# Two of four start-up transposes leave TensorE for the DMA queue, and two sets of weight sums change their place

## The chip, the cores and the metric

The kernel runs on one core of a Trainium2 chip. A core has five engines that run on their own and wait for each other by semaphores: TensorE (PE, matrix products, with a separate record PEld for its weight loads), VectorE (DVE), ScalarE (ACT), GpSimd (POOL) and SyncE (SP), which in this kernel does nothing but issue DMA transfers. Sixteen DMA engines carry out what the queues issue. The metric is the device time of one execution in microseconds (us). Before the change the median of seven runs is 655.6 us (654.49 to 656.85).

## The reference

One input x of 2048 rows (tokens) and 1024 columns goes through two branches that are mixed by a gate per token.

```python
x = A_x
g = _sigmoid((x * gate_w).sum(-1, keepdims=True))
a = _A_ref(x, A_wqkv, A_wo)
b = _B_ref(x, B_w_in, B_w_sp, B_b_sp, B_w_out)
return g * a + (1 - g) * b
```

Branch A is attention with 32 heads of 32 columns, in which a token sees eight tokens only: itself and those 2, 4, ... 14 places before it.

```python
qkv = (x @ wqkv).reshape(B, S, 3, H, Dh).transpose(2, 0, 3, 1, 4)
logits = jnp.einsum('bhsd,bhswd->bhsw', q, kg) * scale
attn = _softmax(logits, axis=-1)
o = jnp.einsum('bhsw,bhswd->bhsd', attn, vg)
return o.transpose(0, 2, 1, 3).reshape(B, S, D) @ wo
```

Branch B is a gated MLP of 3584 hidden columns, whose second half z2 is normalized and mixed over all tokens by the 2048x2048 matrix w_sp.

```python
z = _gelu(jnp.einsum('bsd,df->bsf', x, w_in))
z1 = z[..., :Fh]
z2 = _layernorm(z[..., Fh:], axis=-1)
g = jnp.einsum('ts,bsf->btf', w_sp, z2) + b_sp[None, :, None]
return jnp.einsum('bsf,fd->bsd', z1 * g, w_out)
```

## The kernel before

**Tiles.** A tile of x is 128 tokens; there are sixteen. Nearly every product needs x with its 1024 columns along the partitions, so x is kept turned, as xT: eight blocks of 128 columns by 2048 tokens. A tile reaches xT in one of two ways. A plain load puts it in the buffer xn, TensorE turns its eight 128x128 blocks (`xpose`, L221: eight transposes, and eight copies out of PSUM, in turn on ScalarE L228 and VectorE L230). Or a transposing load (L179, `dma_start_transpose`) writes it turned. Before the change tiles 0 to 3 go the first way and 4 to 15 the second.

**Start.** ScalarE's queue loads the gate's vector gw and the first quarter of wvp, the weights of v for the first three head groups. All else is on SP's queue, in an order that `chained` (L155) fixes: x tile 0, the other three quarters of wvp, x tiles 1 to 3, the transposing loads of tiles 4 and 5, the q and k weights of head group 0 (`load_wqk(0)`), the transposing loads of tiles 6 to 15, `load_wqk(1)`, zeros for the rows ahead of v. All later transfers of SP stand behind these (the proxy at L188). TensorE meanwhile multiplies a cleared buffer six times (`keep_warm`), turns gw into an extra column of wvp, does two more such products, turns tile 0, and runs `vp_tile` (L299) for tiles 0 to 3: eight products of 128x385 that make v and the gate's sum. The turning of the next tile stands inside the product before it (`middle`). Then come `qk_tile` (L290) for 512 tokens at a time, which needs four tiles and the q and k weights, `vp_tile` for further tiles, and small products for the bands of logits (L356, copied by ScalarE at L364). The bands are stored to DRAM by SP and read back in another layout (`load_bands`, L650) for the softmax on VectorE: the maxima L671 to L674, the exponential L662 on ScalarE, weights L683 to L692, then products with v (four slices L708) and their sums L712 to L717.

**Strassen products.** From the gate (L406) on most products are quads: a 2x2 block product in seven products instead of eight (Winograd's form). Their generators are `strassen` (L438) and `chain` (L499), their products line L435. Each needs four sums of weight blocks, made on VectorE (`sums4_steps`, L574, recorded as L577). Between the seven products ScalarE seeds one bank from another (L518) and copies a result to SBUF (L524), and VectorE adds two results (`plus`, L506). Two quads run in step.

**The order of the work.** In the live part a planner writes the order down. It keeps a modelled clock for each engine and each DMA, and at every step `advance(t)` (L764) emits the pieces of other work that are due: pending transfers, exponentials, and on VectorE the earliest among the streams maxima, weights, products, and the list `fill` of sums. A piece of `fill` is due at a modelled time, for instance a modelled landing plus `LATE` = 0.5. On the chip every engine runs its instructions in the order written (`settle`, L211). The planner's clocks start with fixed values at L1001 to L1009.

**The steps that the change touches.** The z2 half of w_in is loaded in two sets (`load_later`, L988; eight pairs of loads each), and when the planner has the last of them landed, four sums go to `fill` at L994. The first set is read by quads at about 186 us, the second by quads some 35 us later. The z1 half runs as seven steps `fp` (loop at L1200), each of two quads; `load_w1` (L841) loads two halves f of w1 for the steps fp and fp + 1 together, `w1_sums` (L1146) makes their sums one step ahead. At the end of a step each quad stores its results (`store`, L1170). In steps 2 to 4 `RAW_AT` places transposing loads of w_sp (`load_raw`, L1109) between the products; eight of them make the first half, and VectorE's sums L1126 to L1130 read all eight.

Of the kernel before, what the change touches and what calls it, by code (L numbers as in the profile page):

```python
# [27 lines left out]
ZC = 448  # L28
# [30 lines left out]
def kernel(  # L59
# [60 lines left out]
    xn = reg(R_OFF, 4 * D).rearrange("p (i d) -> p i d", i=4)  # L120
# [40 lines left out]
    def first_dma(o, i):  # L161
        return chained(nc.sync.dma_start(o, i))

    def load_wqk(g, dma):
        for t in range(2):
            dma(wqk_slots[g][:, t], wq_v[:, :, t * D + g * C:t * D + (g + 1) * C])

    nc.scalar.dma_start(gw_s[:], gw_v)
    def load_wvp(k, dma):
        dma(wvp[:, k:k + 2, 0:VP], wq_v[:, k:k + 2, 2 * D:2 * D + VP])  # L170

    load_wvp(0, nc.scalar.dma_start)
    first_dma(xn[:, 0:1, :], x_v[:, 0:1, :])
    for k in range(2, KT, 2):
        load_wvp(k, first_dma)
    for i in range(1, 4):
        first_dma(xn[:, i:i + 1, :], x_v[:, i:i + 1, :])
    for i in range(4, 16):
        chained(nc.sync.dma_start_transpose(xT[:, :, i * P:(i + 1) * P], x2[i * P:(i + 1) * P, :]))  # L179
        if i == 5:  # L180
            load_wqk(0, first_dma)
    load_wqk(1, first_dma)
    first_dma(bass.AP(tensor=v_d.tensor, offset=v_d.offset, ap=[[C, 16], [(S + 16) * C, NG], [1, C]]), zeros)
# [133 lines left out]
    def keep_warm(n):  # L317
        for _ in range(n):
            inst = nc.tensor.matmul(banks[7], warm[:, 0:P], warm, start=True, stop=True, skip_group_check=True)
            pinned.setdefault(inst.ins.engine, inst.ins.name)  # L320

    keep_warm(6)
    gwT = banks[1][:, 0:KT // 2].bitcast(BF)
    nc.tensor.transpose(gwT, gw_s[:], ident[0:KT, 0:KT])
    nc.vector.tensor_copy(wvp[:, :, VP:VP + 1], gwT.rearrange("p (k o) -> p k o", o=1))
    keep_warm(2)
    xpose(0)
    for i in range(4):
        vp_tile(i, middle=lambda: xpose(i + 1) if i < 3 else None)
    band_at = [0]  # L330
    last_sub = [None]
    last_evac = [None]
# [306 lines left out]
        sync.dma_start(v_t, bass.AP(tensor=v_d.tensor, offset=v_d.offset + (g * (S + 16) + 2) * C, ap=[[NJ * C, P], [1, NJJ * C]]))  # L639


    FR, LATE = 0.4, 0.5
    t_bands, t_v = [FAR] * NG, [FAR] * NG
    sub_end, exp_end = [FAR] * NG, [FAR] * NG
    v_data = [0.0]
# [97 lines left out]
    weighed, fill = [0], []  # L743
# [64 lines left out]
    def wz_sums(p):  # L808
        w = wz[p]
        return sums4_steps(wzs[p], w[0][:, 0:4], w[0][:, 4:8], w[1][:, 0:4], w[1][:, 4:8])  # L810
# [27 lines left out]
    def w1_half(fp, f):  # L838
        return w1_first[:, f] if fp == 0 else w1_pairs[(fp - 1) // 2 % 2][f][:, :, (fp - 1) % 2 * P:((fp - 1) % 2 + 1) * P]

    def load_w1(fp):  # L841
        for f in range(2):
            to = w1_first[:, f] if fp == 0 else w1_pairs[(fp - 1) // 2 % 2][f]
            sync.dma_start(to, win_v[:, :, HF * f + fp * P:HF * f + (fp + (2 if fp else 1)) * P])

# [142 lines left out]
    def load_later(p, at, gap):  # L988
        land = [0.0]

        def landed(t):
            land[0] += 1
            if land[0] == KT:
                fill.extend((t + LATE, 1.05, f) for f in wz_sums(p))  # L994
        for n, f in enumerate(load_wz(p)):
            dma(at + gap * n, 0.65, f, landed, True)

# [143 lines left out]
    z1s_slots = [[free(o + 2048 * r, 2048).rearrange("p (f a t) -> p f a t", f=2, a=2) for r in range(2)] for o in (T1_OFF, R_OFF + 16384)]  # L1141
    zv_slots = [free(R_OFF + 20480 + 1024 * r, 1024, F32) for r in range(2)]

    w1_left = [0]

    def w1_sums(fp):  # L1146
        def one(f):
# [10 lines left out]
    def z1_quad(fp, c):  # L1158
        a, b, s = w1_half(fp, 0), w1_half(fp, 1), ws_slots[fp % 2]
        z1s, vs = z1s_slots[fp == 3][c], zv_slots[c]  # L1160
        lo, hi = slice(512 * c, 512 * c + 512), slice(1024 + 512 * c, 1536 + 512 * c)

        def share(*a):
            last_share[0] = nc.vector.tensor_copy(*a)

        def gelu(f, a, bank):
            act(0.6 + table("gelu"), max(clock["PE"], clock["DVE"] if f + a == 2 else 0.0) + 0.2)
            last_gelu[0] = nc.scalar.activation(z1s[:, f, a, :], bank[:], ACT.Gelu_apprx_tanh)  # L1168

        def store():  # L1170
            dst = z1_d[c].rearrange("p (f t) -> p f t", f=NF)[:, fp:fp + NFH + 1:NFH, :]
            last_store[0] = sync.dma_start(dst, z1s.rearrange("p f a t -> p f (a t)"))

        return chain([a[:, k] for k in K4], [a[:, 4 + k] for k in K4], [b[:, 4 + k] for k in K4],
                     *[[s[:, q, k, :] for k in K4] for q in range(4)],
                     [xT[:, k, lo] for k in K4], [xT[:, 4 + k, lo] for k in K4], [xT[:, 4 + k, hi] for k in K4],
                     *[[x[:, k, lo] for k in K4] for x in xts], vs, gelu, nc.scalar.copy if fp < 2 else share, 512, lean=True, done=store)
# [18 lines left out]
    dma(clock["PE"] + 1.0, 2.9, lambda: load_w1(1), w1_landed(1))  # L1196
    RAW_IN = 3.0
    DRAIN, SUMS = 1, NFH - 2
    RAW_AT = {2: {2: 0, 4: 1, 6: 2}, 3: {4: 3, 6: 4}, 4: {2: 5, 4: 6, 6: 7}}
    for fp in range(NFH):  # L1200
        while w1_left[0]:
            advance(max(clock["PE"], clock["DVE"]) + 0.5)
        if 0 < fp < NFH - 1:
            w1_sums(fp + 1)
        if fp == SUMS:
            fill.extend((clock["PE"] + RAW_IN, 1.15, f) for f in wsp_sums(0, 0))
        late = () if fp else [b[2] for b in bank_roles]
        at = [0]
        run(z1_quad(fp, 0), z1_quad(fp, 1), hooks={3: lambda: mark(late, 512, ZC), **{n: lambda a=a: load_raw(0, a) for n, a in RAW_AT.get(fp, {}).items()}},
            step=lambda: z1_step(fp, at))  # L1210
        if fp == DRAIN:
            drain()
        if fp in (0, 2):
            load_w1(fp + 3)
        if fp == NFH - 3:
            load_rows()
    while fill:
# [426 lines left out]
```

## Time and profile before

| what | value |
|---|---|
| median of seven runs | 655.6 us |
| the profiled execution: its time, its span | 654.91 us, 653.1 us |
| granted TensorE clock | 1.00 in the whole span |
| TensorE busy / waits after the first 2 us | 645.0 us / 3.2 us |
| VectorE busy from 56 to 300 us | nearly all of it; from 80 to 164 it is 78.0 of 84 us |
| share of the chain that ended last | PE 87%, DVE 5%, ACT 4%, DMA 1% |

The span runs from the first to the last instruction, and the execution's own time lies 1.8 us above it. A row of the timeline gives start, length, engine, line of the kernel, operation, out<-in with shapes, a count (merged rows), and in brackets the idle time before it with the work that ended it. A row of an SPq gives the time that SP's sequencer spent on issuing; the transfer lands later. In a list of waits the numbers are the total in us, how often, and the longest.

### The profile page before, as it was taken

Reading aid. Unit: us, or ns where it says so; the run is one execution under the profiler, and the core shown is the slowest. Engines: PE = TensorE matmul, PEld = TensorE weight load, DVE = VectorE, ACT = ScalarE, POOL = GpSimd, SP = SyncE. Lnnn points to the kernel's source line nnn. Section 1 sums busy time; section 2 is a strip of 40 time slices with the busy share of each in tenths; the row PEclk is TensorE's granted clock in tenths of the full one; section 3 lists DMA queues with packets and bytes.
Section 4 is the critical chain, followed back from the end, with each engine's and each line's share of the span. In section 5 each row is a group of like instructions: output and inputs, shape, how many; then the busy total and the mean of one; then the engine's idle time right before and its main releaser. Section 6 shows DMA issues by size and latency. Waiting matters only on the chain.

```text
span 653.1 us, 11411 instructions
## 1 busy us (share of the span) xinstructions
PE 645.0 (99%) x4425; PEld 339.0 (52%) x4425; DVE 517.8 (79%) x820; ACT 298.4 (46%) x652; POOL 6.2 (1%) x15
## 2 busy tenths in 40 slices
PE   8999999999989999999999999999999999999998
PEld 4544467544445555444444444444444444868684
DVE  2533989999899999999898776977659999586862
ACT  4545677766677787799554112111121112202020
POOL 1000000000000000001000000000000000000000
PEclk9999999999999999999999999999999999999999
DMA  9989545697768004247995568559487473455601
GB/s 218 189 212 233 111 101 151 149 232 171 180 181 230 6 1 125 65 129 204 285 222 177 124 161 179 131 160 284 116 187 172 98 152 90 115 143 112 132 30 52
DMA packets 230198, 98.19 MB, mean 150 GB/s; under 512 B 177520, under 2 KB 217088, under 8 KB 230144
## 3 DMA queue, kind: packets, MB, share of 16 engines
q1 hardware_dynamic: 229856, 97.27, 60.8%
q8 instruction: 34, 0.56, 0.4%
q10 hardware_dynamic: 288, 0.20, 0.1%
q14 instruction: 20, 0.16, 0.1%
HBM read 45.10 MB, written 36.61 MB: 125 GB/s over the span
## 4 chain that ended last, share of the span: by engine, by line
PE 87%; DVE 5%; ACT 4%; DMA 1%; issue 1%; SPq 0%; DVEq 0%; ACTq 0%
PE psum_all L435 68%; PE psum_all L1468 8%; PE psum_all L294 7%; PE psum_all L304 3%; ACT arena L870 1%; DVE arena L708 1%; PE psum_all L356 1%; ACT arena L1168 1%; DMA arena<-in_B_w_in_dram 1%; DVE arena L577 1%; DVE psum_all L506 1%; DMA arena<-in_A_x_dram 1%; DVE arena L712 1%; ACT arena L364 0%; ACT arena L815 0%
## 5 line engine op out<-in xcount | busy, mean ns | idle before, releaser
L435 PE MATMUL psum_all<-arena 128*128 128x512 f16 (+6 forms) x2462 | 493.0, 362 | 2.6 <-DVE psum_all L506 1.5
L435 PEld LDWEIGHTS <-arena 128*128 128x128 f16 (+1 forms) x2462 | 239.8, 98 | 248.2 <-issue 4.4
L708 DVE TENSOR_TENSOR arena<-arena,att_A 128x2048 f16<-128x2048 bf16 x64 | 75.2, 1218 | 0.3
L294 PE MATMUL psum_all<-arena 128*128 128x512 bf16 x256 | 57.5, 379 | 0.0
L506 DVE TENSOR_TENSOR psum_all<-psum_all,arena 128x512 f32<-128x512 f32 (+1 forms) x74 | 48.1, 667 | 7.4 <-PE psum_all L435 5.1
L1468 PE MATMUL psum_all<-arena 128*128 128x256 f16 (+1 forms) x468 | 51.7, 273 | 0.0
L1468 PEld LDWEIGHTS <-arena 128*128 128x128 f16 x468 | 45.8, 98 | 5.7 <-issue 0.2
L453 ACT COPY psum_all<-psum_all 128x512 f32<-128x512 f32 (+1 forms) x24 | 12.5, 519 | 67.1 <-PE psum_all L435 66.4
L815 ACT ACTIVATE arena<-psum_all 128x448 bf16<-128x448 f32 x64 | 34.3, 545 | 18.5 <-PE psum_all L435 9.0
L1168 ACT ACTIVATE arena<-psum_all 128x512 bf16<-128x512 f32 x56 | 31.1, 615 | 20.8 <-PE psum_all L435 12.7
L294 PEld LDWEIGHTS <-arena 128*128 128x128 bf16 x256 | 24.4, 98 | 28.4 <-issue 0.2
L712 DVE TENSOR_TENSOR arena<-arena 128x2048 f16<-128x2048 f16 x32 | 38.0, 1216 | 0.0
L364 ACT CAST arena<-psum_all 128x1988 f16<-128x1988 f32 (+3 forms) x25 | 34.0, 1359 | 2.8 <-PE psum_all L356 2.4
L870 ACT ACTIVATE arena<-arena 128x896 bf16<-128x896 bf16 x32 | 30.9, 980 | 0.0
L297 ACT CAST arena<-psum_all 128x512 bf16<-128x512 f32 x32 | 18.8, 586 | 26.5 <-PE psum_all L294 26.4
L577 DVE TENSOR_TENSOR arena<-arena 128x512 f16<-128x512 bf16 (+3 forms) x52 | 25.5, 522 | 5.8 <-DMA arena<-in_B_w_in_dram 5.3
L477 ACT COPY psum_all<-psum_all 128x512 f32<-128x512 f32 (+1 forms) x24 | 12.3, 518 | 37.4 <-PE psum_all L435 36.8
L581 DVE TENSOR_TENSOR arena<-arena 128x1024 f16<-128x1024 f16 (+2 forms) x17 | 12.1, 719 | 19.1 <-PE psum_all L435 15.7
L459 ACT COPY arena<-psum_all 128x512 f32<-128x512 f32 (+1 forms) x24 | 12.7, 533 | 25.1 <-PE psum_all L435 22.8
L464 ACT COPY psum_all<-psum_all 128x512 f32<-128x512 f32 (+1 forms) x24 | 12.4, 517 | 25.8 <-PE psum_all L435 24.8
L518 ACT COPY psum_all<-psum_all 128x512 f32<-128x512 f32 (+1 forms) x37 | 20.6, 567 | 5.7 <-PE psum_all L435 5.0
L304 PE MATMUL psum_all<-arena 128*128 128x385 bf16 x128 | 22.6, 327 | 0.0
(112 smaller groups left out, 521.6 us busy)
## 6 DMA issues: line engine op xcount, KB each, us to landing
arena<-v_d SPq DMA_DIRECT2D x8, 960.0 KB, 6.3
z_d<-arena SPq DMA_DIRECT2D x14, 512.0 KB, 4.3
arena<-z_d SPq DMA_DIRECT2D x14, 512.0 KB, 4.1
zg_d<-arena SPq DMA_DIRECT2D x56, 128.0 KB, 2.2
arena<-zg_d SPq DMA_DIRECT2D x32, 224.0 KB, 3.3
band_d<-arena SPq DMA_DIRECT2D x28, 248.5 KB, 4.0
arena<-in_A_wqkv_dram SPq DMA_DIRECT2D x16, 256.0 KB, 4.6
o_d<-arena SPq DMA_DIRECT2D x4, 1024.0 KB, 6.1
```

Of the source, the lines that this page charges most:

```text
L294: nc.tensor.matmul(ps[:], w[:, t, kt, :], xT[:, kt, 512 * c:512 * (c + 1)], start=(kt == 0), stop=(kt == KT - 1))
L304: nc.tensor.matmul(ps[:, 0:VP + 1], xT[:, kt, i * P:(i + 1) * P], wvp[:, kt, :], start=(kt == 0), stop=(kt == KT - 1))
L364: nc.scalar.copy(dst, src)
L435: nc.tensor.matmul(bank[:, 0:N], lhsT, rhs, start=(start and m == 0), stop=(m == n - 1), skip_group_check=True)
L506: last_add[0] = nc.vector.tensor_tensor(out[:, n], a[:, n], vs, ALU.add)
L577: return [lambda a=a: nc.vector.tensor_tensor(*a) for a in args]
L708: lambda ws=ws, in0=in0, in1=in1: tt(p5[:, ws], in0[:, ws], in1[:, ws], ALU.mult)), False
L712: lambda a=p3[:, ws], b=p3[:, ws.start + 4:ws.stop + 4]: tt(a, a, b, ALU.add)), not n
L815: nc.scalar.activation(z2[:, i + 8 * a, ZC * c:ZC * (c + 1)], bank[:, 0:ZC], ACT.Gelu_apprx_tanh, accum_out=s1[:, 4 * n + c:4 * n + c + 1])
L870: return nc.scalar.activation(junk, src, ACT.Square, accum_out=(s2, s2h)[x][:, n:n + 1])
L1168: last_gelu[0] = nc.scalar.activation(z1s[:, f, a, :], bank[:], ACT.Gelu_apprx_tanh)
L1468: nc.tensor.matmul(bank[:, h], l, r, start=(start and m == 0), stop=(m == len(ab) - 1), skip_group_check=True)
```

## The change

- Only tiles 0 and 1 are loaded plainly and turned by TensorE. Both loads stand ahead of the three quarters of wvp on SP's queue. Tiles 2 and 3 become transposing loads, ahead of the others, and `load_wqk(0)` follows tile 3 instead of tile 5.
- On TensorE tile 0 is turned right after the six warm products, then gw, then tile 1; the two further warm products are gone, and nothing stands inside the first products.
- The z2 sums are due 4.0 after the modelled landing instead of 0.5 (`WZ_LATE`).
- `load_w1(5)` is issued in two parts: half 0 ahead of the sixth product of step 2, half 1 after the step and ahead of that step's two stores, which are kept until then. The transposing load of w_sp number 2 moves from step 2 to step 3, which now has numbers 2, 3 and 4.

```diff
+    PLAIN = 2
     nc.scalar.dma_start(gw_s[:], gw_v)
...
     load_wvp(0, nc.scalar.dma_start)
     first_dma(xn[:, 0:1, :], x_v[:, 0:1, :])
+    first_dma(xn[:, 1:2, :], x_v[:, 1:2, :])
     for k in range(2, KT, 2):
         load_wvp(k, first_dma)
-    for i in range(1, 4):
-        first_dma(xn[:, i:i + 1, :], x_v[:, i:i + 1, :])
-    for i in range(4, 16):
+    for i in range(PLAIN, 16):
         chained(nc.sync.dma_start_transpose(xT[:, :, i * P:(i + 1) * P], x2[i * P:(i + 1) * P, :]))
-        if i == 5:
+        if i == 3:
             load_wqk(0, first_dma)
...
     keep_warm(6)
+    xpose(0)
     gwT = banks[1][:, 0:KT // 2].bitcast(BF)
     nc.tensor.transpose(gwT, gw_s[:], ident[0:KT, 0:KT])
     nc.vector.tensor_copy(wvp[:, :, VP:VP + 1], gwT.rearrange("p (k o) -> p k o", o=1))
-    keep_warm(2)
-    xpose(0)
+    xpose(1)
     for i in range(4):
-        vp_tile(i, middle=lambda: xpose(i + 1) if i < 3 else None)
+        vp_tile(i, middle=None)
...
-    FR, LATE = 0.4, 0.5
+    FR, LATE, WZ_LATE = 0.4, 0.5, 4.0
...
-    def load_w1(fp):
-        for f in range(2):
+    def load_w1(fp, halves=(0, 1)):
+        for f in halves:
...
-                fill.extend((t + LATE, 1.05, f) for f in wz_sums(p))
+                fill.extend((t + WZ_LATE, 1.05, f) for f in wz_sums(p))
...
-    w1_left = [0]
+    w1_left, kept_stores = [0], []
...
-        def store():
+        def store(now=False):
+            if fp == 2 and not now:
+                kept_stores.append(store)
+                return
             dst = z1_d[c].rearrange("p (f t) -> p f t", f=NF)[:, fp:fp + NFH + 1:NFH, :]
...
-    RAW_AT = {2: {2: 0, 4: 1, 6: 2}, 3: {4: 3, 6: 4}, 4: {2: 5, 4: 6, 6: 7}}
+    RAW_AT = {2: {2: 0, 4: 1}, 3: {2: 2, 4: 3, 6: 4}, 4: {2: 5, 4: 6, 6: 7}}
...
-        run(z1_quad(fp, 0), z1_quad(fp, 1), hooks={3: lambda: mark(late, 512, ZC), **{n: lambda a=a: load_raw(0, a) for n, a in RAW_AT.get(fp, {}).items()}},
-            step=lambda: z1_step(fp, at))
+        hooks = {3: lambda: mark(late, 512, ZC), **{n: lambda a=a: load_raw(0, a) for n, a in RAW_AT.get(fp, {}).items()}}
+        if fp == 2:
+            hooks[6] = lambda: load_w1(5, (0,))
+        run(z1_quad(fp, 0), z1_quad(fp, 1), hooks=hooks, step=lambda: z1_step(fp, at))
         if fp == DRAIN:
             drain()
-        if fp in (0, 2):
-            load_w1(fp + 3)
+        if fp == 0:
+            load_w1(3)
+        if fp == 2:
+            load_w1(5, (1,))
+            for f in kept_stores:
+                f(True)
```

## The prediction

> **What bounds the kernel now.** I read the page first, then the waits of TensorE, then the start and the two waits that the change names in the timeline.
>
> ```profile
> span 653.1 us, 11411 instructions
> PE 645.0 (99%) x4425; PEld 339.0 (52%) x4425; DVE 517.8 (79%) x820; ACT 298.4 (46%) x652; POOL 6.2 (1%) x15
> ...
> PE 87%; DVE 5%; ACT 4%; DMA 1%; issue 1%; SPq 0%; DVEq 0%; ACTq 0%
> ```
>
> TensorE is busy 99% of the span, so only its own work and its own waits can shorten the run. The waits of TensorE:
>
> ```profile
> PE psum_all L435 <- DVE psum_all L506: 1.5, 2, 1.4
> PE psum_all L319 <- DVE arena L314: 1.2, 1, 1.2
> PE psum_all L356 <- ACT arena L364: 0.8, 2, 0.6
> PE psum_all L435 <- ACT arena L903: 0.6, 1, 0.6
> PE psum_all L435 <- ACT psum_all L518: 0.3, 1, 0.3
> ```
>
> There are 3.2 us after the start: the most that mended waits can return. The start, in the timeline:
>
> ```profile
> 3.98 1.03 PE L319 MATMUL psum_all<-arena 128*128 128x512 bf16 x2
> ...
> 4.15 3.89 SPq L179 DMA_TRANSPOSE arena<-in_A_x_dram  x2
> ...
> 9.34 15.16 SPq L179 DMA_TRANSPOSE arena<-in_A_x_dram  x10
> ...
> 10.24 0.91 PE L225 MATMUL psum_all<-ident,arena 128*128 128x128 bf16 x8
> ...
> 52.37 1.29 SPq L190 DMA_DIRECT2D att_L<-band_d  x2
> ...
> 56.17 0.29 DVE L671 TENSOR_TENSOR att_m<-att_L 128x256 f16<-128x256 f16 x1 [7.21 <-DMA att_L<-band_d]
> ...
> 59.37 0.63 ACT L662 ACTIVATE att_L<-att_L 128x512 f16<-128x512 f16 x1
> ```
>
> The reader should see SP, not TensorE, as the late one here: from 0.7 to 60.5 us SP issues almost without a gap, and VectorE idles 7.21 us for a load that SP issues at 52.37. The two named waits, and what TensorE pays for each:
>
> ```profile
> 167.40 1.23 DVE L708 TENSOR_TENSOR arena<-arena,att_A 128x2048 f16<-128x2048 bf16 x1
> ...
> 171.41 2.22 DVE L577 TENSOR_TENSOR arena<-arena 128x1792 f16<-128x1792 bf16 x2 [2.79 <-DMA arena<-in_B_w_in_dram]
> ...
> 193.83 6.40 PE L435 MATMUL psum_all<-arena 128*128 128x448 f16 x33 [1.36 <-DVE psum_all L506]
> ...
> 319.27 1.56 DVE L577 TENSOR_TENSOR arena<-arena 128x512 f16<-128x512 bf16 x4 [2.46 <-DMA arena<-in_B_w_in_dram]
> ...
> 323.99 8.36 PE L435 MATMUL psum_all<-arena 128*128 128x512 f16 x38 [0.18 <-DVE psum_all L506]
> ```
>
> **The change, part by part.** The sum is made against the profiled execution: 654.91 us, its span 653.1, 0.7 below the median 655.6.
>
> *TensorE at the start.* Two groups of eight transposes go, 0.69 us from first start to the next line's start (6.85 to 7.54, 8.20 to 8.89): 1.4. Two warm matmuls go (3.98 to 4.80): 0.8. The wait for x tile 1 (6.57 to 6.85) goes: 0.3. Sixteen copies of 0.21 us on ScalarE and VectorE go too; both idle there, so they count nothing. ScalarE's queue keeps its two loads, and POOL's issues none before or after. What is late next are the last weight rows: their load is now behind x tile 1, whose own load landed at 6.8 (issue 2.69 plus 4.1), and they take its place, 0.2 after they are needed. The gate transpose moved behind the first tile hides its 0.19 us copy under the second tile's transposes. Lead: 1.4 + 0.8 + 0.3 - 0.2 = 2.2-2.3; I take 2.2. The transposing loads must keep up: tile 2 issued at 3.2 and landing 5.0 later (the row of tile 4) is there at 8.2, needed at 8.4; tile 3 at 9.1 to 9.9, needed at 9.7; the first q and k weights, issued 1.0 earlier, at 10.6 and 12, needed at 11.1 and 12.8. A slip of up to 1.5 us is covered by what follows.
>
> *SP at the start, which decides.* SP loses two plain issues (0.51 and 0.48 from start to start) and gains two transposing ones (1.35 in the steady stretch 16.4 to 24.5): 2.7 - 1.0 = 1.7 us later at everything behind them: wqk 1, the zeros, the v and band stores, the wvr and wqk 2 loads, the loads of the first group's bands. On the way one wait of SP, 0.6 us for the band copy L364 at 38, falls away because TensorE leads. So the band load, and VectorE's L671, come 1.1 us later: L674 ends at 57.41 + 1.1 = 58.5, and the exponential L662 can start at 58.6. It has 59.37 now, because ScalarE is busy for TensorE until then. Behind it in ScalarE's order stands L518 (59.90), the copy that seeds the bank for the third product: TensorE waits for it. So of the 2.2 only 59.37 - 58.6 = **0.7 us** gets past 60 us. Bounds: if both new transposing loads issue as the slowest did (2.49), SP is 4.1 later, 3.5 after the 0.6, and the start loses 1.7; if the shorter plain backlog saves the 2.9 us by which five early transposing issues exceed 1.31, SP is earlier than now and the whole 2.2 passes. I take 0.7, from the steady row: nine of the twelve issues lie nearer to it than to 2.49.
>
> In these rows a transposing load of one x tile holds SP for 1.31 us, a plain one for 0.41 to 0.47. [...]
>
> *The z2 sums.* They are entered 3.5 us later in the planner's list (4.0 for 0.5 after the modelled landing). Work from its other streams takes their place: three slices of L708 (3.49 for three) and the maxima L671 to L674. The weights land at 171.3; sums placed after 168.6 + 3.5 find them, so the 2.79 wait goes. What is late next is the next group's band load: its second half is issued at 169.8 and lands 2.4 later, 172.2. After two slices (170.9) the maxima wait 1.3. VectorE gains 2.79 - 1.3 = 1.5; TensorE had stopped at 192.47 (187.01 + 5.46) and can take back only its **1.36**. Bounds: 0.4 if the maxima come after one slice, 1.36 if nothing waits. I take 1.35, the nearer. The second set of sums (four near 1.08, 210.3 to 215.8) moves by as much, to 219 at most; its first is read by the second product of the first quad of the second set, near 220.8 (the additions of that round start at 223.79, two steps of 1.5 later). That margin is its cover.
>
> *The w1 loads.* The two loads for the sixth step (0.98 and 1.36 to issue, landing 6.1 and 6.8 later) pass two stores (1.2) and one transposing load of the spatial weights (2.1), issuing at 307.9 in place of 311.4: they land by 316 and the 2.46 wait at 316.8 goes. TensorE gets its **0.18**. The stores wait longer; their slots are reused two steps on. The spatial load moved a step on has the same issues ahead of the last one as now, so the sums L1126 at 335.9 keep a margin of about 1 us (last landing 332.9 less 3.84, plus 5.8). If that cover goes, VectorE waits for up to one such issue, 2.1.
>
> *After that.* From 194 to 324 TensorE waits 0.5 in all, and ScalarE waits 7.7 us for TensorE between 194 and 262, so the others follow an earlier TensorE; from 324 to the end it has no wait. Sum: 0.7 + 1.35 + 0.2 = **2.25 us**: 652.7 for the profiled run, **653.4** for the median. Own range, with the start between 0 and 1.5 and the sums between 0.9 and 1.36: 652.4 to 654.5.
>
> The six warm matmuls of 512 columns take 2.74 us, 0.46 each; from 5.6 on matmuls of 385 columns start 0.16 apart. The granted clock in the profile's rows is 1.00 all the while. [...]
>
> **The rivals.**
> 1. SP is not late: 0.7 becomes 2.2, time 655.6 - 3.75 = 651.9. For it: the early long issues follow plain loads, of which there are fewer. Against: transfers keep the DMA share near 1.0 from 4 to 28 us, and two more transposing loads do not lessen that.
> 2. The wait changes its name: the maxima stand ahead of the slices and wait for the band load, 0.4 for 1.35: 655.6 - 1.3 = 654.3.
> 3. SP at its worst: 1.35 + 0.2 - 1.7 = -0.15: 655.7. For it: the second transposing issue took 2.49, and now it stands where both do.
> 4. Slower: the second set of z2 sums, 3.5 later, falls among the additions L506 of the next quads, and TensorE waits behind each: up to 4 x 1.08 = 4.3, 655.6 - 2.25 + 4.3 = 657.7. From 2.25 on it decides the sign. For it: VectorE has 1.0 us of waits between 200 and 256. Against: the margin of several us above.
>
> **How the numbers follow.** A difference of 0.2% (1.3 us) is about what a measurement here can tell from none. Forecast 0.50 (0.44 of it faster), rival 1 0.12, rival 2 0.13 (half and half at the bound), rival 3 0.10 (same, a little slower), rival 4 0.15. Faster 0.60, same 0.23, slower 0.17. The range takes in rivals 1 to 3 with a margin for the reordered list: 651.7 to 656.4; rival 4 stays out.
>
> **What would show it.** Right: the L294 matmuls start near 11.1 rather than 13.3; L671 near 57.3 and L662 near 58.6, with ScalarE idle ahead of it; no DMA wait of L577 near 171 and 319, perhaps one of L671 near 172; no wait of TensorE near 193. Wrong: L662 after 59.4, TensorE idle before 15, or a new wait on L506 after 210.

## The result, and the profile after

The changed kernel takes **652.99 us** in the median of 15 runs (650.85 to 654.33). The kernel before, run beside it on the same chip, takes 655.45 us (36 runs). The ratio is 0.9959, with a 95% interval of 0.9950 to 0.9967: 2.5 us faster. The profiled execution of the changed kernel took 652.99 us, with a span of 651.2 us (before: 654.91 and 653.1).

The head of the page and the summary of its chain of waits:

```profile
span 651.2 us, 11356 instructions
PE 643.6 (99%) x4407; PEld 338.1 (52%) x4407; DVE 516.1 (79%) x812; ACT 296.5 (46%) x644; POOL 6.2 (1%) x15
...
PE 85%; DVE 5%; ACT 5%; DMA 3%; issue 1%; SPq 1%; DVEq 0%; ACTq 0%
```

TensorE is still what bounds the kernel. Its busy time fell by 1.4 us (18 matmuls and transposes fewer), and DMA now has 3% of the chain in place of 1%. Two of the waits of TensorE after the change moved by more than 0.1 us (total, times, longest):

```profile
PE psum_all L435 <- ACT psum_all L518: 0.8, 2, 0.5
...
PE psum_all L435 <- DVE psum_all L506: 0.6, 1, 0.6
```

The wait on L506, VectorE's addition, fell from 1.5 to 0.6. The wait on L518, ScalarE's seeding copy, rose from 0.3 to 0.8. The rows that say where both come from are in the timeline, first the opening stage:

```profile
11.29 2.97 PE L294 MATMUL psum_all<-arena 128*128 128x512 bf16 x13
...
53.22 1.28 SPq L190 DMA_DIRECT2D att_L<-band_d  x2
...
56.98 0.29 DVE L671 TENSOR_TENSOR att_m<-att_L 128x256 f16<-128x256 f16 x1 [7.58 <-DMA att_L<-band_d]
...
58.25 0.63 ACT L662 ACTIVATE att_L<-att_L 128x512 f16<-128x512 f16 x1 [0.77 <-DVE att_L L674]
58.79 0.58 ACT L518 COPY psum_all<-psum_all 128x512 f32<-128x512 f32 x1
...
59.42 1.02 PE L435 MATMUL psum_all<-arena 128*128 128x512 f16 x4 [0.52 <-ACT psum_all L518]
60.37 0.65 PE L356 MATMUL psum_all<-arena 32*64 32x71 bf16 x56
```

The two rows of the kernel before that these are held against:

```profile
13.28 2.97 PE L294 MATMUL psum_all<-arena 128*128 128x512 bf16 x13
...
61.67 0.65 PE L356 MATMUL psum_all<-arena 32*64 32x71 bf16 x56
```

The q and k products start at 11.29 in place of 13.28, so TensorE leads by 1.99 us. The load of att_L, however, is issued 0.85 us later than before. VectorE's maxima follow at 56.98, ScalarE idles 0.77 us for them before the exponential L662, and L518 stands behind that. TensorE waits 0.52 us there; the band product L356 starts at 60.37 in place of 61.67. **1.3 us of the 2.0 pass.** From there to 186 us the lead stays at 1.3.

The stage of the z2 sums, timeline and then chain of waits (start, length):

```profile
166.78 2.36 DVE L708 TENSOR_TENSOR arena<-arena,att_A 128x2048 f16<-128x2048 bf16 x2
...
171.67 0.29 DVE L671 TENSOR_TENSOR att_m<-att_L 128x256 f16<-128x256 f16 x1 [2.53 <-DMA att_L<-band_d]
...
173.96 4.22 DVE L577 TENSOR_TENSOR arena<-arena 128x1792 f16<-128x1792 bf16 x4
...
191.15 1.16 DVE L506 TENSOR_TENSOR psum_all<-psum_all,arena 128x448 f32<-128x448 f32 x2
...
191.82 5.38 PE L435 MATMUL psum_all<-arena 128*128 128x448 f16 x26 [0.65 <-DVE psum_all L506]
...
192.21 2.35 DVE L712 TENSOR_TENSOR arena<-arena 128x2048 f16<-128x2048 f16 x2
```

```profile
163.08 6.07 DMA band_d<-arena
...
169.21 2.38 DMA att_L<-band_d
```

VectorE's rows before the change, for the same additions L506:

```profile
192.02 1.22 DVE L712 TENSOR_TENSOR arena<-arena 128x2048 f16<-128x2048 f16 x1
193.15 1.16 DVE L506 TENSOR_TENSOR psum_all<-psum_all,arena 128x448 f32<-128x448 f32 x2
```

The sums L577 no longer wait, but VectorE still does: 2.53 us for the band load where it waited 2.79 us for the weights. The wait changed its name. Yet TensorE goes on at 191.82 in place of 193.83, 2.0 us ahead of before. Then 0.3 us is given back, because two slices of L712 now stand ahead of the next pair of L506: at 262 us TensorE is 1.7 ahead. The wait of 0.18 on L506 near 324, behind the w1 sums, is gone. The last step of the kernel is 1.95 us earlier (650.12 to 648.17). So 1.3 from the start, 0.7 at 192 us, 0.3 given back and 0.2 at 324 us make 1.9, which is what the two profiled executions differ by; their medians differ by 2.5.

### The profile page after: what moved, and what is told of

The parts are those of the page before. It is cut to its first block, busy times and chain, and to the rows that moved or that the text cites. A ratio compares the mean times of both kernels' runs of the same rounds, so it can differ in the third digit from the quotient of the medians.

```text
span 651.2 us, 11356 instructions
## 1 busy us (share of the span) xinstructions
PE 643.6 (99%) x4407; PEld 338.1 (52%) x4407; DVE 516.1 (79%) x812; ACT 296.5 (46%) x644; POOL 6.2 (1%) x15
## 4 chain that ended last, share of the span: by engine, by line
PE 85%; DVE 5%; ACT 5%; DMA 3%; issue 1%; SPq 1%; DVEq 0%; ACTq 0%
PE psum_all L435 68%; PE psum_all L1477 8%; PE psum_all L294 4%; PE psum_all L304 3%; ACT arena L870 1%; DVE arena L708 1%; ACT arena L1168 1%; DMA band_d<-arena 1%; PE psum_all L356 1%; DMA att_L<-band_d 1%; SPq L190 1%; DVE psum_all L506 1%; DVE arena L712 1%; DMA arena<-in_A_wqkv_dram 1%; ACT arena L364 1%
## 5 line engine op out<-in xcount | busy, mean ns | idle before, releaser
L708 DVE TENSOR_TENSOR arena<-arena,att_A 128x2048 f16<-128x2048 bf16 x64 | 75.3, 1218 | 0.3
L506 DVE TENSOR_TENSOR psum_all<-psum_all,arena 128x512 f32<-128x512 f32 (+1 forms) x74 | 48.3, 667 | 7.8 <-PE psum_all L435 3.9
L712 DVE TENSOR_TENSOR arena<-arena 128x2048 f16<-128x2048 f16 x32 | 37.9, 1216 | 0.0
L364 ACT CAST arena<-psum_all 128x1988 f16<-128x1988 f32 (+3 forms) x25 | 34.0, 1359 | 2.6 <-PE psum_all L356 2.0
L577 DVE TENSOR_TENSOR arena<-arena 128x512 f16<-128x512 bf16 (+3 forms) x52 | 25.4, 521 | 2.7 <-DMA arena<-in_A_wqkv_dram 2.3
L518 ACT COPY psum_all<-psum_all 128x512 f32<-128x512 f32 (+1 forms) x37 | 20.6, 570 | 5.4 <-PE psum_all L435 4.8
L418 DVE TENSOR_TENSOR arena<-arena 128x2048 f16<-128x2048 bf16 x8 | 9.4, 1222 | 17.1 <-DMA arena<-in_A_x_dram 17.0
## 6 DMA issues: line engine op xcount, KB each, us to landing
band_d<-arena SPq DMA_DIRECT2D x28, 248.5 KB, 4.6
```

What stands on the lines that cost most here:

```text
L364: nc.scalar.copy(dst, src)
L506: last_add[0] = nc.vector.tensor_tensor(out[:, n], a[:, n], vs, ALU.add)
L518: last_seed[0] = nc.scalar.copy(Y[:, n], X[:, n])
L577: return [lambda a=a: nc.vector.tensor_tensor(*a) for a in args]
L708: lambda ws=ws, in0=in0, in1=in1: tt(p5[:, ws], in0[:, ws], in1[:, ws], ALU.mult)), False
L712: lambda a=p3[:, ws], b=p3[:, ws.start + 4:ws.stop + 4]: tt(a, a, b, ALU.add)), not n
```

## The experiments

Two theories were set against each other. **A:** two transfers decide what passes: the load of att_L at 53 us, which comes late in SP's list, and the load of att_L at 169 us, which waits for band stores. **B:** those transfers are not what decides; the lead goes to the order of the work, and the waits do not follow the loads. The experiments ran on three other chips, four kernels on each. On all three the kernel before is slower and scatters more (medians 658.6, 659.0 and 658.9 us, single runs from 656.4 to 662.6) than on the first chip (655.45, 654.5 to 658.0), so tenths can't be read off these times. The traces carry the verdicts, with two limits. A trace is one execution, which can lie far from its kernel's median (654.43 against 656.92 for the sums at 2.0, 657.73 against 655.84 for the four tiles, below), and no trace of the kernel before was taken on these chips, so edited kernels stand in for it. In some edited kernels the line numbers are up to three higher.

### One part at a time

**The start alone** (loads, transposes and warm matmuls of the change, on the kernel before):

```
+    PLAIN = 2
...
+    first_dma(xn[:, 1:2, :], x_v[:, 1:2, :])
...
-    for i in range(4, 16):
+    for i in range(PLAIN, 16):
...
+    xpose(0)
...
-    keep_warm(2)
-    xpose(0)
+    xpose(1)
```

> The kernel before with the start of the changed kernel alone. Theory A (SP sets what of the start passes 60 us): TensorE leads by 2.0 us at the first q product (11.3 instead of 13.3), the band load and L671 come near 57.0, the exponential L662 near 58.2, TensorE waits about 0.5 for the seed copy L518, and only 1.3 us are left behind it; the time falls by about 1.3 us (ratio 0.998), and VectorE's wait for the z2 weights (2.8) and TensorE's wait near 192 (1.4) stay. Rival B (the lead passes whole): 2.0 us, ratio 0.997.

Measured: 658.54 us, ratio 0.9996 (0.9973 to 1.0018). The timeline of this kernel:

```profile
58.16 0.29 DVE L671 TENSOR_TENSOR att_m<-att_L 128x256 f16<-128x256 f16 x1 [7.77 <-DMA att_L<-band_d]
...
60.60 1.02 PE L435 MATMUL psum_all<-arena 128*128 128x512 f16 x4 [2.12 <-ACT psum_all L518]
```

The lead is there (the first q product is at 10.87), but the maxima come at 58.16, and TensorE stands 2.12 us. A kernel with the old start on the same chip (the w1 part alone, below) has its first q product at 13.65 and the band product at 62.05; here it is at 61.55. So 0.5 of 2.8 us passed in this execution.

**The z2 sums alone** (`t + LATE` becomes `t + WZ_LATE`, 4.0, on the kernel before):

> The kernel before with the z2 sums due 4.0 after the modelled landing, nothing else. Theory A (the wait changes its name): VectorE's wait for the z2 weights near 171 goes, and L671 waits about 2.5 us for the band load att_L instead; TensorE's wait near 193 falls from 1.4 to about 0.65, with a further 0.3 near 197; the time falls by 0.4 to 0.7 us (ratio 0.999). Rival B (the prediction's size): the wait near 193 goes whole, 1.35 us, ratio 0.998.

Measured: 657.45 us, ratio 0.9987 (0.9966 to 1.0007). Its timeline:

```profile
59.87 0.29 DVE L671 TENSOR_TENSOR att_m<-att_L 128x256 f16<-128x256 f16 x1 [10.71 <-DMA att_L<-band_d]
...
62.30 1.02 PE L435 MATMUL psum_all<-arena 128*128 128x512 f16 x4 [1.22 <-ACT psum_all L518]
...
174.91 0.29 DVE L671 TENSOR_TENSOR att_m<-att_L 128x256 f16<-128x256 f16 x1 [3.51 <-DMA att_L<-band_d]
...
195.07 2.24 PE L435 MATMUL psum_all<-arena 128*128 128x448 f16 x11 [1.01 <-DVE psum_all L506]
```

Two things follow. The load of att_L can be late with the old start too (59.87, and a wait of 1.22), so a late att_L is not the change's doing alone. And VectorE waits 3.51 us for the band load, as in the full change: the new name of the wait comes from this part. What the part is worth does not show on this chip: TensorE goes on at 195.07 here, at 194.97 with the start alone and at 195.73 with the w1 part alone, and the last two have the old order of the sums.

**The w1 loads alone** (order of w1, stores and spatial weights, on the kernel before):

> The kernel before with the moved w1(5) loads, kept stores and moved w_sp load alone. Theory A: VectorE's wait of 2.5 us near 317 goes, TensorE gets its 0.2 us, the time falls by 0.2 us and cannot be told from none (ratio 0.9995 to 1.000). Rival B (the wait is worth more than the 0.18 recorded for TensorE, because additions behind it come earlier): 0.5 us or more, ratio 0.9992 or less.

Measured: 658.65 us, ratio 0.9995 (0.9977 to 1.0013). VectorE's wait for w1 (2.46 before) is gone, and so is TensorE's wait on L506 near 326. With the old w1 order on that chip, the two kernels above have waits of VectorE of 3.0 and 3.3, and of TensorE of 0.68 and 0.99. But part of that comes back a little later, at the sums of the spatial weights (L1126, here L1127):

```profile
338.88 1.23 DVE L1127 TENSOR_TENSOR arena<-arena 128x2048 f16<-128x2048 bf16 x1 [1.38 <-issue]
...
353.82 2.53 PE L436 MATMUL psum_all<-arena 128*128 128x512 f16 x11 [0.49 <-DVE psum_all L507]
```

The three traces with the old w1 order have no such wait of TensorE. Of those with the new order only the one on the first chip has none; in the ten others VectorE waits 1.1 to 2.1 us there and TensorE 0.3 to 1.0 behind it. So the part is worth 0.2 us on the first chip and, against those two executions, 0.2 to 0.5; the times are too wide to show it.

**All parts, with tiles 2 and 3 turned by TensorE again** (so SP issues two transposing loads fewer):

```
-    for i in range(PLAIN, 16):
+    for i in range(2, 4):
+        first_dma(xn[:, i:i + 1, :], x_v[:, i:i + 1, :])
+    for i in range(4, 16):
...
-        vp_tile(i, middle=None)
+        vp_tile(i, middle=lambda: xpose(i + 1) if i in (1, 2) else None)
```

> The changed kernel, but tiles 2 and 3 are loaded plainly again and turned by TensorE inside the products of tiles 1 and 2; load_wqk(0) follows tile 5 again. The two warm products stay out, and tiles 0 and 1 stay ahead of wvp. Theory A (SP sets it): TensorE leads the kernel before by 1.0 rather than 2.0 at the first q product, but SP is not late, L671 stays near 56.2 and L662 follows ScalarE's own work; the whole 1.0 passes 60 us, so it loses only 0.3 us on the changed kernel. Rival B (the transposing loads bring the gain): it loses 1.0 us on the changed kernel.

Measured: 655.84 us, ratio 0.9959 (0.9940 to 0.9978), the same ratio as the full change. TensorE's q products start at 12.80, 0.85 ahead of the old start on that chip (13.65); the band product starts at 61.20 in place of 62.05. All of that smaller lead passes: L671 came at 57.74, in time, and TensorE did not wait for L518 there. Further on this trace goes against the z2 part: although the sums have their new place, TensorE waits 2.81 us on L506 and goes on at 194.94, after VectorE has waited for two loads of att_L (3.79 and 1.22). It is the execution of 657.73, 1.9 above the median. By the ratios, turning two tiles by transposing loads has no clear worth.

### The load of att_L at 53 us

**The zeros off SP's list** (their store into v_d moved to ScalarE's queue, on the kernel after):

```
+    nc.scalar.copy(omg[:, 0:1], cm05[0:16, 0:1])
+    nc.scalar.dma_start(bass.AP(tensor=v_d.tensor, offset=v_d.offset, ap=[[C, 16], [(S + 16) * C, NG], [1, C]]), zeros)
...
-    first_dma(bass.AP(tensor=v_d.tensor, offset=v_d.offset, ap=[[C, 16], [(S + 16) * C, NG], [1, C]]), zeros)
```

> The kernel after, with the store of zeros into v_d taken off the tail of SP's opening list (its issue held SP 1.82 us there) and issued from ScalarE's queue. Theory A (SP's list of transfers decides at 58 us): SP comes about 1.8 us earlier to its first band stores, the load of att_L goes out 1 to 2 us earlier, L671 starts before 56.5, L662 no longer waits for VectorE, TensorE's wait on L518 near 59 (0.52 in the kernel after) is gone and the whole lead of about 2.0 passes; 0.5 to 0.7 us faster than the kernel after. Rival B (the lead is lost at 60 us whatever SP does, to the order of ScalarE's work): L671 comes earlier, but TensorE still waits about 0.5 on L518.

Measured: 657.04 us, ratio 0.9981 (0.9965 to 0.9996); the kernel after beside it: 655.98. SP in this kernel's timeline, and then in that of the kernel after on the same chip:

```profile
27.62 3.08 SPq L191 DMA_DIRECT2D v_d<-arena  x3
...
54.07 1.29 SPq L191 DMA_DIRECT2D att_L<-band_d  x2
```

```profile
27.52 2.52 SPq L162 DMA_DIRECT2D v_d<-arena  x1
30.14 1.56 SPq L190 DMA_DIRECT2D v_d<-arena  x3
...
53.19 1.28 SPq L190 DMA_DIRECT2D att_L<-band_d  x2
```

Theory A's expectation failed. One issue of 2.52 us was taken off, the next three stretched from 1.56 to 3.08, and the load of att_L went out later, not earlier. Counting issues, as the prediction did, does not give SP's time between 26 and 53 us. The run is no clean test of the issue itself, though. This kernel also lost 1.7 us at the start, where a transpose waited for ScalarE's copies: its first q product is at 12.54, against 10.91 in the kernel after on that chip. SP was 1.0 ahead at the first band stores (30.80 against 31.81) and 1.9 behind at the next (39.41 against 37.49); from 26 to 45 us it waited 3.6 us for what ScalarE writes, against 2.8. So the late start may have taken back what the missing issue gave. In all 14 traces that stretch, from the second pair of wqk weights to the load of att_L, takes 26.0 to 29.2 us. What its long issues wait for, beyond that, the traces do not settle.

**The load of att_L ahead of the gate's stores** (on the kernel after):

```
-    sync.dma_start(... g_d ..., g_s[:])
-    gate_dma = sync.dma_start(... og_d ..., omg_h[:])
...
+    dma(0.0, 0.1, gate_stores)
     next_v(1)
     load_wqk_later(3, 0.0)
+    dma(0.0, 0.1, lambda: sync.dma_start(g_att[:], ...))
```

> The kernel after, with the two loads of att_L put ahead of the two gate stores in SP's order (in the kernel after the gate stores hold SP from 52.18 to 53.22), and the small load of g_att put behind the loads of v and weights. In seven executions so far in which ScalarE waited there, TensorE's band product went on 2.43 to 2.44 us after the start of L671. Theory A (the load of att_L decides when the lead passes 60 us): L671 starts 0.5 to 1.0 earlier than in the kernel after on this chip, TensorE's wait on L518 near 59 shrinks by as much (to 0.5 or less), the time by up to that; L687 gets no wait for g_att. Rival B (the load waits for the band stores' landing, not for SP's turn): the load's own wait takes the place, L671 less than 0.3 earlier, nothing gained.

Measured: 656.96 us, ratio 0.9976 (0.9952 to 1.0001). The timeline of this kernel, and of the kernel after beside it:

```profile
53.17 1.29 SPq L190 DMA_DIRECT2D att_L<-band_d  x2
...
56.89 0.29 DVE L674 TENSOR_TENSOR att_m<-att_L 128x256 f16<-128x256 f16 x1 [6.87 <-DMA att_L<-band_d]
...
59.33 1.02 PE L438 MATMUL psum_all<-arena 128*128 128x512 f16 x4 [0.53 <-ACT psum_all L521]
...
62.98 0.22 DVE L690 TENSOR_TENSOR att_r<-att_s,g_att 128x64 f16<-128x64 f32 x1 [1.66 <-DMA g_att<-g_d]
```

```profile
54.08 1.29 SPq L190 DMA_DIRECT2D att_L<-band_d  x2
...
57.90 0.29 DVE L671 TENSOR_TENSOR att_m<-att_L 128x256 f16<-128x256 f16 x1 [7.99 <-DMA att_L<-band_d]
...
60.34 1.02 PE L435 MATMUL psum_all<-arena 128*128 128x512 f16 x4 [1.76 <-ACT psum_all L518]
```

The mechanism is as Theory A has it: load, maxima and product each come 0.9 to 1.0 earlier, and TensorE's wait shrinks from 1.76 to 0.53. The expectation that L687 (here L690) would get no wait was wrong: the small load of g_att, put last, came 1.66 late, the additions behind it were late, and TensorE waited 1.3 us on them near 65. The gain was spent 5 us later. The expected gain in time did not come: the median is 1.6 above that of the kernel after beside it (655.34), with intervals that just overlap.

The 14 traces of all kernels together say what decides this stage. "q" is the start of the first q product, "att_L" SP's load, "L671" the maxima, "wait" TensorE's wait on the seeding copy, "L356" the start of the band product (us):

| kernel, start | q | att_L | L671 | wait | L356 | L356 - L671 |
|---|---|---|---|---|---|---|
| before, old | 13.28 | 52.37 | 56.17 | 0 | 61.67 | 5.50 |
| z2 alone, old | 13.47 | 54.26 | 59.87 | 1.22 | 63.26 | 3.39 |
| w1 alone, old | 13.65 | 51.90 | 55.86 | 0 | 62.05 | 6.19 |
| four tiles turned | 12.80 | 53.56 | 57.74 | 0 | 61.20 | 3.46 |
| zeros moved, new | 12.54 | 54.07 | 57.98 | 0.27 | 61.37 | 3.39 |
| after, new | 11.29 | 53.22 | 56.98 | 0.52 | 60.37 | 3.39 |
| after, 2nd execution | 10.91 | 53.19 | 57.17 | 1.09 | 60.56 | 3.39 |
| after, 3rd execution | 11.19 | 54.08 | 57.90 | 1.76 | 61.29 | 3.39 |
| start alone, new | 10.87 | 54.20 | 58.16 | 2.12 | 61.55 | 3.39 |
| z2 loads earlier, new | 11.38 | 54.21 | 59.26 | 2.71 | 62.65 | 3.39 |
| sums at 2.0, new | 11.46 | 53.28 | 57.20 | 0.57 | 60.59 | 3.39 |
| z2 loads later, new | 11.45 | 53.93 | 58.20 | 1.80 | 61.60 | 3.40 |
| bands first, new | 11.40 | 53.17 | 56.89 | 0.53 | 60.28 | 3.39 |
| both, new | 11.30 | 51.67 | 55.25 | 0 | 59.48 | 4.23 |

Wherever TensorE waits, the band product starts 3.39 or 3.40 us after the maxima, in ten executions with L671 anywhere from 56.89 to 59.87. Whatever TensorE has gained by then is lost. In the one execution with a new start and an early att_L (the last row) nothing is lost: 59.48. SP's turn is not all that makes the load late: from its issue to the maxima it takes 3.6 to 4.3 us in twelve of the rows, but 5.05 and 5.61 in two (z2 loads earlier, z2 alone).

### The load of att_L at 169 us

**The z2 loads spaced by 5 us in place of 6** (on the kernel after: `load_later(0, clock["PE"] + 4.0, 5.0)`):

> The kernel after, with the z2 weight loads spaced by 5 instead of 6 us in the planner's time, so that all of them are issued earlier. Theory A (the wait changed its name: the band stores and the load of att_L stand behind the z2 loads in the DMA queues): with the loads out of the way L671's wait near 172 (2.53 in the kernel after) falls below 1 and TensorE's wait on L506 near 192 (0.65) falls by as much as the sums move, to below 0.3; up to 0.6 us faster than the kernel after. Rival B (L671 waits for the band stores' own way through DRAM, whatever else is in the queues): the 2.5 and the 0.65 stay.

Measured: 660.48 us, ratio 1.0019 (1.0003 to 1.0036). The timeline:

```profile
155.92 4.75 SPq L190 DMA_DIRECT2D att_L<-band_d  x2
...
185.55 0.27 PE L356 MATMUL psum_all<-arena 32*64 32x64 bf16 x16 [1.76 <-ACT arena L364]
```

Both theories missed: this kernel is 4.5 us slower than the kernel after beside it (655.98), and the two intervals lie apart. Loads that come earlier stand ahead of the previous group's transfers: the pair of att_L loads goes out at 155.92 and holds SP 4.75 us (151.21 and 3.91 in the kernel after on the first chip; in the kernel after beside it SP is past that pair by 154.54), the band copies stall, and TensorE waits 1.76 us for one of them (L364) and later 2.9 us on L506. Not all that this trace loses is the edit's: at 62 us, long before the z2 loads (the first goes out at 122.62 in the kernel after on the first chip), TensorE is already 2.1 behind the kernel after on that chip (62.65 against 60.56); of the 4.7 by which it is behind at 190 us, 2.6 are left for the edit.

**The sums due 2.0 us after landing in place of 4.0** (on the kernel after: `WZ_LATE` 2.0):

> The kernel after, with the z2 sums due 2.0 instead of 4.0 us after the planned landing. Theory A (0.65 of TensorE's wait on L506 near 192 is left because VectorE does the four sums after L671 and so waits 2.53 for att_L instead of 2.79 for the weights): sums put ahead of L671 wait about 1 for their weights and then cover the wait for att_L; TensorE's wait near 192 falls to 0.3 or less. Rival B (whatever the order, VectorE has some 2.5 us to wait there because the transfers end when they end): VectorE's waits at 166 to 176 still sum to 2.3 or more, and TensorE's wait is 0.5 or more.

Measured: 656.92 us, ratio 0.9966 (0.9945 to 0.9987). The timeline:

```profile
171.60 1.09 DVE L577 TENSOR_TENSOR arena<-arena 128x1792 f16<-128x1792 bf16 x1 [2.36 <-DMA arena<-in_B_w_in_dram]
172.82 0.29 DVE L671 TENSOR_TENSOR att_m<-att_L 128x256 f16<-128x256 f16 x1
...
192.30 1.16 DVE L506 TENSOR_TENSOR psum_all<-psum_all,arena 128x448 f32<-128x448 f32 x2
192.98 5.27 PE L435 MATMUL psum_all<-arena 128*128 128x448 f16 x27 [1.40 <-DVE psum_all L506]
```

Rival B is right here: the sums ahead of the maxima wait 2.36, the maxima then find their data, and TensorE waits 1.40. VectorE has done its other work by 169.2, and neither load is there before 171. Which of the two it waits for first makes no difference to it: its slices L708 start at 186.30, and at 186.28 in the kernel after on the first chip. TensorE is later here for another reason. A slice of L712 stands ahead of the first L506 again, as in the kernel before, and L506 starts at 192.30 in place of 191.15. So this run also shows what the place of L506 in VectorE's order is worth: 1.15 us.

**The z2 loads 3 us later** (on the kernel after: `clock["PE"] + 7.0, 6.0`). The planner then puts three slices of L708 ahead of the maxima, and the sums far behind them.

> The kernel after, with the z2 weight loads 3 us later in the planner's time, so that the four band stores of the sixth group are issued ahead of the last two pairs of loads and the sums fall some 5 us later, behind the next L687. Theory A (L671's wait near 172, 2.5 and 4.2 in two executions of the kernel after, comes from band stores that stand behind the z2 loads): that wait falls below 1.5, the sums wait less than 0.5 for their weights, TensorE's wait on L506 near 192 (0.65 and 1.70) falls below 0.4; 0.4 to 1.2 us faster than the kernel after. Rival B (the stores take their 6 us whatever is ahead of them): L671 waits 2.5 or more, TensorE's wait stays above 0.6.

Measured: 654.68 us, ratio 0.9933 (0.9906 to 0.9959); the kernel after beside it 655.34. The timeline:

```profile
168.19 3.50 DVE L708 TENSOR_TENSOR arena<-arena,att_A 128x2048 f16<-128x2048 bf16 x3
173.09 0.29 DVE L671 TENSOR_TENSOR att_m<-att_L 128x256 f16<-128x256 f16 x1 [1.41 <-DMA att_L<-band_d]
...
177.27 4.21 DVE L577 TENSOR_TENSOR arena<-arena 128x1792 f16<-128x1792 bf16 x4
...
192.75 5.57 PE L435 MATMUL psum_all<-arena 128*128 128x448 f16 x27 [0.35 <-DVE psum_all L506]
```

The numbers are those of Theory A (1.41, no wait of the sums, 0.35), but not its reason. The last band store still took 8.26 us to land, and the maxima start at 173.09, against 173.29 in the kernel after on that chip: the load is hardly earlier. VectorE waits less because a third slice (1.1 us) stands ahead, and because it arrived 0.9 later. So the stores' landing is not cured by issuing them ahead of the last two pairs of z2 loads; the order of VectorE's work is what helped. (One of those pairs went out 1.5 us behind the store, at 163.65, so the two still overlap, and what slows the store stays open.) The median is 0.7 below that of the kernel after, and the ranges overlap: not shown to be faster.

**Both edits**, loads of att_L first and z2 loads later:

> Both edits together (loads of att_L ahead of the gate stores, z2 loads 3 us later). Theory A: the two gains add up, 1 to 2 us faster than the kernel after, 3 to 4.5 faster than the kernel before. Rival B: within 0.3 of the kernel after.

Measured: 653.96 us, ratio 0.9923 (0.9896 to 0.9950). The timeline:

```profile
57.17 0.63 ACT L665 ACTIVATE att_L<-att_L 128x512 f16<-128x512 f16 x1
...
59.48 0.65 PE L357 MATMUL psum_all<-arena 32*64 32x71 bf16 x56
...
61.72 0.23 DVE L690 TENSOR_TENSOR att_r<-att_s,g_att 128x64 f16<-128x64 f32 x1 [1.36 <-DMA g_att<-g_d]
...
64.27 2.10 PE L438 MATMUL psum_all<-arena 128*128 128x512 f16 x8 [0.87 <-DVE psum_all L509]
```

ScalarE has no wait at L665, and the band product starts at 59.48, the earliest of all. The late g_att takes 0.87 back. The median is 1.4 us below that of the kernel after beside it, but the two ranges overlap (653.32 to 655.91 and 653.65 to 655.95), and so do the intervals: the best of these kernels, not shown to be faster than the change.

### The changed kernel again, on two other chips

> The kernel after, unchanged, beside the three that edit it, on their chip. Both theories: 0.995 to 0.997 of the kernel before. Theory A: the lead of TensorE at its first band product (some 2 us) is cut by a wait on L518 near 59 that is as long as L671 comes late, 0.3 to 2.1 us by the execution. Rival B: that wait is 0.5 in every execution.

> The kernel after, unchanged, beside the three that edit it, on their chip. Theory A: 2.0 to 3.0 us faster than the kernel before; TensorE's second half of the first band product starts 2.44 us after L671, and its wait near 192 goes with L671's near 172. Rival B: these two waits do not go together.

Measured: 655.98 us, ratio 0.9956 (0.9941 to 0.9971), and 655.34 us, ratio 0.9931 (0.9904 to 0.9958). The gain is there on three chips. The two rows in the table above bear out Theory A for the first wait: 1.09 and 1.76, as late as the maxima were. The second wait, in the third execution:

```profile
173.29 0.29 DVE L671 TENSOR_TENSOR att_m<-att_L 128x256 f16<-128x256 f16 x1 [3.60 <-DMA att_L<-band_d]
...
193.44 4.82 PE L435 MATMUL psum_all<-arena 128*128 128x448 f16 x23 [1.03 <-DVE psum_all L506]
```

Over the three executions of the same kernel VectorE's wait at L671 is 2.53, 3.60 and 4.21, and TensorE's near 192 is 0.65, 1.03 and 1.70: they go together.

## Why the prediction was right, and where it was not

The time was 652.99 for a forecast of 653.4. The steps, one by one.

*TensorE's lead at the start*, 2.2: measured 1.99. The weights of the last rows were late by 0.28 and 0.34, 0.6 rather than 0.2 in all; the rest was a little better than worked out, also because the second group of transposes had taken 0.74 (8.20 to 8.94) and not 0.69. The two warm matmuls that went cost nothing that the trace shows: 32 matmuls of 385 columns take 5.70 us from 5.59 to 11.29, with 0.62 of waits, 0.16 each as before, at a granted clock of 1.00. That is 2.4 columns per ns, against 1.1 in the six warm matmuls (512 columns in 0.46 us each, at a granted clock of 1.00 too); what makes those slower is not shown. With six of them as with eight, the first matmuls of 385 columns start at 5.59 and run at the faster rate.

*What of it passes 60 us*, 0.7: measured **1.3**; this is the term that was mis-sized, though its mechanism held (L662 with ScalarE idle ahead of it, behind the load of att_L). Two parts of it. SP was 0.85 late at the load rather than 1.1; the two transposing loads more put it 1.1 late at the second wqk weights (24.54 to 25.65) where 1.7 was worked out. And TensorE was taken to follow L662, but in the kernel before L518 ended some 0.2 us before TensorE wanted it, so TensorE gained the 1.1 of L662 and this 0.2. The worst case of rival 3 (a loss of 1.7) did not come, but the start alone shows how near it is: 0.5 of 2.8 passed there.

In the profile of the changed kernel a transposing load takes 1.31 us of SP in the median, and a plain one of the same tile 0.41. They land 3.9 and 3.0 us after issue (3.8 and 4.1 in the kernel before): the two kinds are near each other in landing, but not in what they take of the queue that issues them.

*The z2 sums*, 1.35 for the removed wait: measured **0.7** in TensorE's wait (1.36 to 0.65). The step that failed is "after two slices (170.9) the maxima wait 1.3". Only two slices in all, not three, stood ahead of the maxima; VectorE was there at 169.14 and waited 2.53. VectorE gained 0.87 at the end of its L708 slices, not 1.5. What made up for it had not been seen: the first pair of L506 now stands ahead of a slice of L712 in VectorE's order, worth another 1.13 (in the run with the sums at 2.0 the slice is ahead again, and L506 is 1.15 later). Together L506 came 2.0 earlier.

The sum had a fault of book-keeping too. It added the start's lead and the whole of TensorE's removed wait. But a TensorE that arrives 1.3 earlier waits 1.3 longer if VectorE does not come earlier too, and VectorE's wait ends with a load, at 171.41 before and 171.67 after. So TensorE's gain at 192 us is VectorE's 2.0; the 1.3 of lead and the 0.7 of wait are two pieces of it. That 0.7 + 1.35 comes to 2.05 as well is luck. That the start alone would have lost its lead here is worked out, not shown: in its own run TensorE reached the place 0.6 earlier than with the w1 part alone on the same chip and went on 0.8 earlier (194.97 against 195.73), but VectorE's load was 0.8 earlier there as well (172.54 against 173.31).

*The w1 loads*, 0.2: right on the first chip (0.18). On the others the removed wait was longer (0.68 and 0.99), but the margin of about 1 us that was to cover the sums L1126 was gone: VectorE waited 1.1 to 2.1 us there, the most being the 2.1 that had been named for this case, and TensorE 0.3 to 1.0.

*The parts together.* Alone, in medians, they gave 0.0, 1.1 and -0.1 us, 1.0 in all, where the whole change gave 2.5 to 3.6 on the chips on which it ran. Each of the three intervals takes in no change at all, and together they are wide enough for the difference. So the times do not show what a part is worth; what is said of the parts rests on the traces.

*The rivals.* Rival 2, the wait that changes its name, is what happened in the z2 stage; it gave less of a loss than it priced (1.35 to 0.4) only because of the order of L506. Rival 4 did not happen: from 194 to 324 us TensorE has no wait on L506 in any of the three executions of the changed kernel. Rivals 1 and 3 lie on both sides of what SP does, and the table shows that one kernel moves between them from execution to execution: 0.5 to 1.8 us of wait.

## What to carry to other kernels

Before adding two gains, ask what ends the wait further on: if it is a transfer or an engine that does not follow the first gain, the two gains can't be added. Here TensorE got at 192 us the 2.0 us by which L506 came earlier, not 1.3 of lead and 1.36 of wait. A lead that is won at the start is worth only what the latest load lets through (1.3 of 2.0 here, 0.5 of 2.8 with the start alone), so look for the next place where the leading engine waits on a transfer, and price that place, with its slack, in the same trace. A wait that is moved to other work stays a wait when that work waits for a load that lands at the same time (2.79 us became 2.53, for loads that let VectorE go on at 171.41 and 171.67); count which work is left that needs no load.

## What the runs showed that was not expected

- With 2.52 us of issue taken out of SP's list, the next three issues took 3.08 in place of 1.56; SP was 1.0 ahead at the band stores that follow, and the load that mattered went out 0.9 later. The kernel had also lost 1.7 us at its start, so the two are not told apart.
- Band stores of 248.5 KB took 6.4 to 8.5 us (medians) to land between 155 and 172 us, those of 71 KB 2.4 to 4.8. It stayed so where the last two pairs of z2 loads were issued behind them (8.26 in the chain of that kernel).
- In three executions of the same program, on three chips, the maxima that wait for att_L start at 56.98, 57.17 and 57.90, and TensorE's wait there is 0.52, 1.09 and 1.76. These waits differ by up to 1.24 us, 0.2% of the time, so a difference of 0.1% between two such kernels can't be read from one trace of each.
- Three chips ran the kernel before 0.5% slower than the first (658.6 to 659.0 against 655.45) with a wider scatter; the gain of the change was there on each on which it ran.
